# A packed-attention, maxout and softplus kernel: the first batch and the second attention of batch 1 written as 313 steps in one order

## The chip, the cores and the metric

The kernel runs on one core of one Trainium2 chip. Five engines work at the same time, each through its own list of instructions in order: TensorE (PE, matmuls into PSUM), VectorE (DVE), ScalarE (ACT), GpSimd (POOL) and SyncE (SP, which here only issues DMAs). They wait for each other by semaphores. The metric is the device time of one execution in microseconds (us), and of several executions the median.

## The reference

Attention over 8 batches and 8 heads, 576 rows of 64, with 32 packed queries in between, then two feed-forward layers over all 4608 tokens:

```python
def sm_attn(qq, kk, vv):
    s = scale * np.matmul(qq, kk.transpose(0, 1, 3, 2))
    s = s - np.max(s, axis=-1, keepdims=True)
    a = np.exp(s)
    a = a / (np.sum(a, axis=-1, keepdims=True) + 1e-09)
    return np.matmul(a, vv)
p_packed = sm_attn(p, k, v)                 # 32 packed rows per head
out = sm_attn(q, p_packed, p_packed)        # then 4608 tokens x 512
h = np.maximum(np.maximum(x @ w1, x @ w2), x @ w3)    # 512 -> 768
x = h @ w_out                                         # 768 -> 512
g = log1p(exp(x @ w_in))                              # 512 -> 2048
return g @ w_out2                                     # 2048 -> 512
```

q, k, v and p are single precision; the weights are double precision and are read as pairs of 32-bit words.

## The kernel before

**Stages.** For each of the eight batches: K and Q are turned so that the head dimension lies on the partitions; the first attention's scores, maximum, exponential, transposes and values give the packed values; the second attention's scores and softmax follow; the packed values are multiplied into the weights of layer 1 ("packed weights", `ps_w`, L370), so that the second attention's values and layer 1 are one product; 18 units of layer 1 (6 slices by 3 weights, `layer1_unit`) are combined by maximum; 4 units of layer 2 write the tokens to DRAM (`x2d`). After the last batch layers 3 and 4 run over all tokens (L808, L854 to L856); the change doesn't touch them.

**Splits.** Products of single precision are done in three: `split` (L106) writes a rounded copy on ScalarE (`hi`, L107) and the rest (`lo`, L108) on VectorE or GpSimd; `three` (L391) does hi x hi, hi x lo and lo x hi.

**Weights.** A block of double-precision weights is loaded raw (512 KB, pool `stp` with five buffers) and narrowed by three instructions: ScalarE (`rebase`, L82), GpSimd (low bits, L94) and VectorE (combining, L97). 18 blocks are layer 1's (`wsb`), 6 are w_out's (`wo`).

**Pools that set waits.** `mm` has four PSUM buffers, and every product of the attention and of layers 1 and 2 takes one; `rx` has five buffers for pieces of K and Q (one piece is two heads), `stp` five for raw weights.

**Order.** Batch 0, and the attention of batch 1, are a list of names, one per step: `L` loads a piece, `T` turns it, `LW`/`LO` load weights, `N`/`SO` narrow them, `PP` transposes P, `S`, `E`, `Vv`, `PT` are the first attention, `A`, `W`, `X` the second, `PW` packs weights, `L1`, `L1S`, `L2` are the layers:

```python
order = """
    Lk00 Lk01 Lk02 LW00 LO0 Lk03 ID LW01 LW02 Tk00 Lq00 SO0 Lv0 Lq01 Lq02 LW10 Lp0
    ...
for name in order.split():
    steps[name]()
```

A step emits all its instructions, for every engine, at its place. A planner then orders each engine's list, by the place in the text and its own estimate of when an operand is ready. From batch 1's layer 1 on, `pinned` fixes TensorE's order, and `in_turn` SyncE's.

In batches 0 and 1 K, and in batch 0 Q, are turned by TensorE as matmuls with the identity (`BY_PE`, L199) and copied out of PSUM by ScalarE (L207, L212); the rest of Q and K by VectorE (L220, L223). V of batch 0 is loaded on ScalarE's queue, all else on SyncE's.

## Time and profile before

| what | us |
|---|---|
| median of 3 runs | 1285.69 (1284.87 to 1288.09) |
| profiled execution | 1286.58 |
| its span | 1284.4 |
| TensorE busy in the span | 1248.1 (97%) |
| VectorE, ScalarE, GpSimd busy | 667.6, 453.1, 124.3 |

The span is the time from the first to the last recorded instruction. Windows cut it into stretches and give each engine's busy time in them; a timeline lists instructions in order, with the idle time before them in brackets and what ended it. The granted clock is 1.00 at TensorE's higher level (2.4 GHz) and 0.50 at the lower (1.2 GHz). A name like `ps_k<-ident,kraw` reads: written tile, then operands. A profile counts each single-precision turn or score twice, since TensorE runs it in two passes.

### The profile page before, as it was taken

To read this page: it belongs to the slowest core of one execution; us is meant where nothing else is said; L and a number is where in the kernel's file an instruction comes from. 1 tells how busy PE (TensorE), PEld (TensorE's weight loads), DVE (VectorE), ACT (ScalarE), POOL (GpSimd) and SP (SyncE) were. 2 spreads that over 40 slices of the span, in tenths; PEclk is the share of its full clock that TensorE was granted. 3 is DMA by queue.
4 is the path that set the end of the run, shared out by engine and by line. 5 is a ranking of instruction groups with operands and counts; after the bars stand their busy time and mean duration, and the time that the engine had idled before them with its cause. 6 is when DMAs were issued, how large, how long until landed. Compare 5 with 4: busy or idle time off the path is not lost.

```text
span 1284.4 us, 23494 instructions
## 1 busy us (share of the span) xinstructions
PE 1248.1 (97%) x9952; PEld 1128.2 (88%) x9952; DVE 667.6 (52%) x949; ACT 453.1 (35%) x629; POOL 124.3 (10%) x116
## 2 busy tenths in 40 slices
PE   4889999999999999999999999999999999999998
PEld 3679899998989998999999999999999999999997
DVE  1656566675756657686453444544444435444432
ACT  3543434444343434553333322233232222332221
POOL 2242313131222212000000000000000000000000
PEclk9999999999999999999999999999999999999999
DMA  9972849677686725967556556555565554655641
GB/s 265 239 205 90 216 137 238 172 209 195 194 233 183 177 87 181 366 220 287 205 178 225 196 211 217 188 209 207 186 211 186 205 205 172 230 192 186 212 181 49
DMA packets 82121, 255.10 MB, mean 199 GB/s; under 512 B 12128, under 2 KB 47200, under 8 KB 72544
## 3 DMA queue, kind: packets, MB, share of 16 engines
q1 hardware_dynamic: 76240, 242.46, 59.1%
q10 hardware_dynamic: 5776, 11.14, 2.6%
q8 instruction: 78, 1.28, 0.4%
q14 instruction: 27, 0.22, 0.1%
HBM read 211.62 MB, written 41.94 MB: 197 GB/s over the span
## 4 chain that ended last, share of the span: by engine, by line
PE 91%; DVE 1%; issue 0%; ACT 0%; DMA 0%; POOLq 0%; SPq 0%; DVEq 0%
PE ps L808 28%; PE ps L391 28%; PE acc L856 10%; PE acc L855 10%; PE acc L854 10%; PE ps_w L370 2%; PE ps_s L247 1%; PE ps_v L301 1%; PE ps_e L281 1%; DVE wu L713 0%; DVE m L416 0%; ACT wc L107 0%; DMA out_dram<-o 0%; PE ps_t L231 0%; POOLq L938 0%
## 5 line engine op out<-in xcount | busy, mean ns | idle before, releaser
L808 PE MATMUL ps<-x2hi,wc 128*128 128x256 f32 x2016 | 370.5, 281 | 0.0
L808 PEld LDWEIGHTS ps<-x2hi,wc 128*128 128x128 f32 x2016 | 316.1, 190 | 2.7
L808 PE MATMUL ps<-x2lo,wc 128*128 128x256 f32 x1008 | 283.7, 281 | 0.0
L856 PE MATMUL acc<-w2hi,glo 128*128 128x512 f32 x576 | 224.9, 391 | 0.0
L855 PE MATMUL acc<-w2lo,ghi 128*128 128x512 f32 x576 | 224.8, 390 | 0.0
L854 PE MATMUL acc<-w2hi,ghi 128*128 128x512 f32 x576 | 224.3, 389 | 0.0
L808 PEld LDWEIGHTS ps<-x2lo,wc 128*128 128x128 f32 x1008 | 191.4, 190 | 2.8
L837 ACT ACTIVATE h<-h 128x1024 f32<-128x1024 f32 x72 | 76.3, 1060 | 286.7 <-DVE h L834 286.7
L831 DVE TENSOR_TENSOR h<-h,ps 128x512 f32<-128x512 f32 x72 | 49.5, 688 | 226.4 <-PE ps L808 225.5
L108 DVE TENSOR_TENSOR glo<-h,ghi 128x1024 fp32r<-128x1024 f32 x72 | 88.1, 1223 | 85.0 <-ACT ghi L107 85.0
L391 PE MATMUL ps<-a2hi,pwhi 128*128 128x288 f32 x576 | 128.1, 304 | 0.2 <-DVE pwlo L108 0.2
L856 PEld LDWEIGHTS acc<-w2hi,glo 128*128 128x128 f32 x576 | 108.1, 188 | 23.0 <-DVE glo L108 0.2
L854 PEld LDWEIGHTS acc<-w2hi,ghi 128*128 128x128 f32 x576 | 108.3, 188 | 20.3
L855 PEld LDWEIGHTS acc<-w2lo,ghi 128*128 128x128 f32 x576 | 108.1, 188 | 20.5
L391 PE MATMUL ps<-a2hi,pwlo 128*128 128x288 f32 x576 | 124.0, 297 | 0.3 <-issue 0.3
L391 PE MATMUL ps<-a2lo,pwhi 128*128 128x288 f32 x576 | 123.7, 296 | 0.1
L416 DVE TENSOR_TENSOR m<-ps,m 128x576 f32<-128x576 f32 x96 | 72.3, 753 | 63.5 <-PE ps L391 51.4
L391 PEld LDWEIGHTS ps<-a2hi,pwhi 128*128 128x128 f32 x576 | 92.4, 190 | 13.1 <-ACT m L414 5.9
L108 POOL TENSOR_TENSOR hlo<-m,hhi 128x576 fp32r<-128x576 f32 x48 | 69.3, 1444 | 335.7 <-ACT hhi L107 325.1
L830 ACT ACTIVATE h<-ps 128x256 f32<-128x256 f32 x72 | 27.6, 383 | 188.4 <-PE ps L808 188.4
L391 PEld LDWEIGHTS ps<-a2lo,pwhi 128*128 128x128 f32 x576 | 93.0, 189 | 0.3 <-DVE a2lo L108 0.3
L391 PEld LDWEIGHTS ps<-a2hi,pwlo 128*128 128x128 f32 x576 | 93.1, 189 | 0.2 <-DVE pwlo L108 0.2
(86 smaller groups left out, 1510.6 us busy)
## 6 DMA issues: line engine op xcount, KB each, us to landing
wc<-wic SPq DMA_DIRECT2D x66, 1792.0 KB
qraw<-in_q_dram SPq DMA_DIRECT2D x112, 140.0 KB
wic<-wc SPq DMA_DIRECT2D x8, 1792.0 KB
kraw<-in_k_dram SPq DMA_DIRECT2D x96, 140.0 KB
wraw<-in_moe_w_dram SPq DMA_DIRECT2D x18, 512.0 KB
x2d<-xs ACTq DMA_DIRECT2D x32, 288.0 KB
xu<-x2d SPq DMA_DIRECT2D x36, 256.0 KB
out_dram<-o SPq DMA_DIRECT2D x136, 64.0 KB
```

Of the source, the lines that this page charges most:

```text
L108: engine.tensor_tensor(out=lo, in0=src, in1=hi.bitcast(F32), op=ALU.subtract)
L247: nc.tensor.matmul(ps[G][cols, hh, :HS], w[rows, cols], x[rows, g, hh * HS : hh * HS + HS], start=True, stop=True,)
L370: nc.tensor.matmul(ps[cols, G, : units * P].rearrange("p (w x) -> p w x", w=units), ppT[n][rows, cols], wsb[rows, 4 * c : 4 * c + units, g ...
L391: nc.tensor.matmul(o, w, xx, start=first, stop=last)
L416: nc.vector.tensor_tensor(out=m, in0=ps[:, :, :HS], in1=ms[n, f], op=ALU.max)
L808: nc.tensor.matmul(out, l, r, start=(i == 0), stop=(i == len(terms) - 1))
L830: nc.scalar.activation(out=h[:, 3], in_=pa[:, 0], func=AF.Copy)
L831: add(out=h[:, 0:5:4], in0=h[:, 3:4].to_broadcast([P, 2, HC]), in1=pb, op=ALU.add)
L837: nc.scalar.activation(out=g, in_=g, func=AF.Softplus)
L854: nc.tensor.matmul(ps, ghi[:, i, cols], whi, start=first, stop=False)
L855: nc.tensor.matmul(ps, ghi[:, i, cols], wlo, start=False, stop=False)
L856: nc.tensor.matmul(ps, glo[:, i, cols], whi, start=False, stop=last)
```

## The change

Batch 0 and the second attention of batch 1 are written again as 313 names. A step is now a generator that yields between its parts, so that a name stands once for each part: `Tk00` is first the turn on TensorE and, at its second place, the copy on ScalarE. The text runs inside `tc.manual_schedule` for all five engines: each engine's list is what the text says, and the planner doesn't reorder it. From layer 1 of batch 1 on, the text is what it was but for one split.

These things differ in what the text says. K, P and Q of batch 0 come first on SyncE's queue, V too stands there (it was on ScalarE's), and the weights come behind. Forty matmuls of the identity with itself (`idle_turns`, counts in `lead`) are put ahead of ten steps of TensorE; they write a part of a PSUM tile that nothing reads. `on_gpsimd` names nine operations that run on GpSimd: of the second attention's softmax and splits, and two w_out splits. The six maxout splits of batch 0, and four w_out splits, have their rest on VectorE now. Batch 1's second scores (`A1`) come after the first unit of layer 2. The turns of batch 2's K stand after the list, outside it. And in the last batch the last maxout split has its rest on VectorE, by the new argument of `maxout_steps`.

SyncE, from the start. Before (`kraw`, `qraw`, `praw`, `vt` are pieces of K, Q, P and V, `wraw` and `woraw` raw weights):

```order
L146 DMA kraw<-in_k_dram 96x2x384 x3
L468 DMA wraw<-in_moe_w_dram 128x4x256
L455 DMA woraw<-in_moe_w_out_dram 128x1024
L146 DMA kraw<-in_k_dram 96x2x384
L468 DMA wraw<-in_moe_w_dram 128x4x256 x2
L146 DMA qraw<-in_q_dram 96x2x384 x3
```

SyncE, from the start, now:

```order
L171 DMA kraw<-in_k_dram 96x2x384 x2
L204 DMA praw<-in_p_dram 128x1x64 x2
L171 DMA kraw<-in_k_dram 96x2x384 x2
L171 DMA qraw<-in_q_dram 96x2x384 x3
L195 DMA vt<-in_v_dram 96x8x384
L565 DMA wraw<-in_moe_w_dram 128x4x256
L171 DMA qraw<-in_q_dram 96x2x384
```

The fourth piece of K moved ahead of all weights, and Q and V follow it directly but for one weight block.

TensorE, from the start to the second scores of batch 0. Before (`ps_k` are turns, `ps_s` scores, `ps_e` transposes of exponentials, `ps_v` values, `ps_t` small transposes):

```order
L199 MATMUL ps_k<-ident,kraw 64x96 x48
L199 MATMUL ps_k<-ident,qraw 64x96 x12
L231 MATMUL ps_t<-ident,praw 128x128
L247 MATMUL ps_s<-vT,pT 32x288 x16
L231 MATMUL ps_t<-ident,praw 128x128
L281 MATMUL ps_e<-ident,e_285 96x128 x6
L281 MATMUL ps_e<-ident,e_290 96x128 x6
L301 MATMUL ps_v<-vt,e1T 32x64 x48
L231 MATMUL ps_t<-ident,pp 128x128
L199 MATMUL ps_k<-ident,qraw 64x96 x36
L247 MATMUL ps_s<-vT,ppT 32x288 x16
```

The same place now, up to the values:

```order
L162 MATMUL ps_k<-ident 128x128 x11
L228 MATMUL ps_k<-ident,kraw 64x96 x12
L262 MATMUL ps_t<-ident,praw 128x128
L228 MATMUL ps_k<-ident,kraw 64x96 x36
L162 MATMUL ps_s<-ident 128x128 x2
L283 MATMUL ps_s<-vT,pT 32x288 x16
L228 MATMUL ps_k<-ident,qraw 64x96 x24
L327 MATMUL ps_e<-ident,e_264 96x128 x6
L327 MATMUL ps_e<-ident,e_288 96x128 x6
L228 MATMUL ps_k<-ident,qraw 64x96 x12
L162 MATMUL ps_v<-ident 128x128
L354 MATMUL ps_v<-vt,e1T 32x64 x48
```

Two of the three Q turns that stood behind the values moved ahead of them (the third comes behind the packed values' transpose), and rows with the identity alone are new.

VectorE, eight rows of layer 1 of batch 0. Before (`m` is a maximum over units, `wsb` a combined weight block, `pwlo` the rest of packed weights, `hlo` of the maxout):

```order
L416 TENSOR_TENSOR m<-ps_706,m 128x576
L97 SCALAR_TENSOR_TENSOR wsb<-wsb,wraw 128x512
L416 TENSOR_TENSOR m<-ps_721,m 128x576
L97 SCALAR_TENSOR_TENSOR wsb<-wsb,wraw 128x512 x2
L108 TENSOR_TENSOR pwlo<-ps_w,pwhi 128x1024
L97 SCALAR_TENSOR_TENSOR wsb<-wsb,wraw 128x512 x2
L416 TENSOR_TENSOR m<-ps_786,m 128x576
L97 SCALAR_TENSOR_TENSOR wsb<-wsb,wraw 128x512
```

VectorE, eight rows of that layer now:

```order
L507 TENSOR_TENSOR m<-ps_637,m 128x576
L108 SCALAR_TENSOR_TENSOR wsb<-wsb,wraw 128x512 x2
L507 TENSOR_TENSOR m<-ps_688,m 128x576
L108 SCALAR_TENSOR_TENSOR wsb<-wsb,wraw 128x512
L124 TENSOR_TENSOR hlo<-m,hhi 128x576
L124 TENSOR_TENSOR pwlo<-ps_w,pwhi 128x1024
L108 SCALAR_TENSOR_TENSOR wsb<-wsb,wraw 128x512 x2
L507 TENSOR_TENSOR m<-ps_755,m 128x576
```

The maxout split's rest stands on VectorE now, between combinings of weights and the packed weights' rest.

The diff, cut to its core. Most functions are only divided at `yield`; one of each kind is shown.

```diff
+    def low_bits(raw):
         top = raw.bitcast(mybir.dt.uint8)[:, :, 3]
         nc.gpsimd.tensor_scalar(
-            out=low, in0=top, scalar1=1.0 / 32, scalar2=-31.0 / 64, op0=ALU.mult, op1=ALU.add
-        )
+            out=raw[:, :, 0],
+            in0=top,
+            scalar1=1.0 / 32,
+            scalar2=-31.0 / 64,
+            op0=ALU.mult,
+            op1=ALU.add,
+        )
+
+    def narrow(raw, x):
+        low_bits(raw)
+        combine(raw, x)
...
     def split(src, hi, lo, engine=nc.vector):
+        for _ in split_steps(src, hi, lo, engine):
+            pass
+
+    def split_steps(src, hi, lo, engine=nc.vector):
         nc.scalar.activation(out=hi, in_=src, func=AF.Copy)
+        yield
         engine.tensor_tensor(out=lo, in0=src, in1=hi.bitcast(F32), op=ALU.subtract)
...
+    ps1, psv, ps2, on_gpsimd, lead = {}, {}, {}, set(), {}
+
+    def every(steps):
+        for _ in steps:
+            pass
+
+    def idle_turns(name, ps):
+        for _ in range(lead.get(name, 0)):
+            nc.tensor.transpose(ps[:, 384:], ident, ident)
...
     def transpose_kq(n, g, which):
+        every(turn_steps(n, g, which))
+
+    def turn_steps(n, g, which):
...
             ps = mm.tile([P, 2, 512], F32, tag="mm", name="ps_k")
+            idle_turns(f"T{which}{n}{g}", ps[:, 0])
             for i in range(NI):
...
+    def square_steps(src, tag, kept, n, scale=1.0):
 
         ps = mm.tile([P, 2, 512], F32, tag="mm", name="ps_t")
+        idle_turns(f"{'PP' if tag == 'pT' else 'PT'}{n}", ps[:, 1])
         nc.tensor.transpose(ps[:, 0, :P], src, ident)
+        yield
         t = tp.tile([P, P], F32, tag=tag, name=tag)
         nc.scalar.activation(out=t, in_=ps[:, 0, :P], func=AF.Copy, scale=scale)
-        return t
+        kept[n] = t
...
+    def scores1(n):
+        ps1[n] = scores(pT.pop(n), vT.pop((n, "k")), f"S{n}")
+
+    def exp1_steps(n, G):
+        ps = ps1[n][G]
         mx = tp.tile([P, 1], F32, tag="mx", name="mx")
         nc.vector.tensor_reduce(
             out=mx, in_=ps[:, :, :HS], axis=AX.XY, op=ALU.max, negate=True
         )
+        yield
...
+    def values(n):
+        ps = psv[n] = mm.tile([P, 2, 512], F32, tag="mm", name="ps_v")
+        idle_turns(f"V{n}", ps[:, 0])
...
+    def gpsimd_if(name):
+        return nc.gpsimd if name in on_gpsimd else nc.vector
...
-        nc.vector.tensor_tensor(
+        yield
+        gpsimd_if(f"AX{n}{G}.sb").tensor_tensor(
             out=s, in0=s, in1=mx.unsqueeze(2).to_broadcast([P, T, 32]), op=ALU.subtract
         )
+        yield
...
+    def attention2_steps(n, G):
+        yield from exp2_steps(n, G)
+        yield
+        yield from weight_steps(n, G)
...
+    def x_steps(n, G):
         hi = a2p.tile([P, S], F32R, tag="a2hi", name="a2hi")
         lo = a2p.tile([P, S], F32R, tag="a2lo", name="a2lo")
-        split(a2.pop((n, G)), hi, lo)
+        yield from split_steps(a2.pop((n, G)), hi, lo, gpsimd_if(f"X{n}{G}"))
...
-    def layer1(n, f):
-        for w in range(3):
-            layer1_unit(n, f, w)
-
     def layer1_split(n, f):
+        every(maxout_steps(n, f, nc.vector if (n, f) == (B - 1, F1 - 1) else nc.gpsimd))
+
+    def maxout_steps(n, f, engine):
         m = ms.pop((n, f)).rearrange("p h c -> p (h c)")
         hhi = hx.tile([P, S], F32R, tag="hx", name="hhi")
         hlo = hx.tile([P, S], F32R, tag="hx", name="hlo")
-        split(m, hhi, hlo, nc.gpsimd)
+        yield from split_steps(m, hhi, hlo, engine)
...
-    def split_wo(f, t):
-        x = mp.tile([P, S], F32, tag="m", name="wo32")
-        rebase(t, x[:, :DM])
-        narrow(t, x[:, :DM])
-        split(x[:, :DM], wo_hi[:, f], wo_lo[:, f], nc.gpsimd)
+    def split_wo_steps(f):
+        t = wo_raw[f]
+        x = mp.tile([P, S], F32, tag="m", name="wo32")[:, :DM]
+        rebase(t, x)
+        yield
+        combine(t, x)
+        yield
+        yield from split_steps(x, wo_hi[:, f], wo_lo[:, f], gpsimd_if(f"SO{f}"))
...
-    order = """
-        Lk00 Lk01 Lk02 LW00 LO0 Lk03 ID LW01 LW02 Tk00 Lq00 SO0 Lv0 Lq01 Lq02 LW10 Lp0
...
-    for name in order.split():
-        steps[name]()
...
+    def once(fn, *args):
+        fn(*args)
+        yield
+
+    def opening(name):
+        a, num = name.rstrip("0123456789"), name[len(name.rstrip("0123456789")) :]
+        i = [int(c) for c in num]
+        if a in ("Lk", "Lq"):
+            return once(load_raw, i[0], i[1], a[1])
...
+            "AX": attention2_steps,
+            "X": x_steps,
...
+    on_gpsimd.update("""AX00.sb AX00.mu AX01.mu SO5 SO0 AX10.sb AX11.sb AX10.mu X11""".split())
+    lead.update({"Tk00": 11, "S0": 2, "V0": 1, "PT0": 2, "A0": 2, "Tk10": 12, "Tk13": 2, "PP1": 4, "S1": 3, "U0": 1})
+    order = """
+            Lk00 Lk02 Lp0 Lk01 Lk03 Lq00 Tk00 PP0 Tk00 Lq03 Tk02 PP0 Tk01 Tk02 Lq02 Lv0
+            LW01 Tk03 Tk01 Lq01 LW02 LW10 Tk03 LW00 S0 Lk10 Tq00 SX00 SX01 SX00 Tq02
...
+    E = mybir.EngineType
+    under_way = {}
+    make_identity(nc, ident)
+    with tc.manual_schedule(engines={E.PE, E.DVE, E.Activation, E.Pool, E.SP}):
+        for name in order.split():
+            if name not in under_way:
+                under_way[name] = opening(name)
+            next(under_way[name], None)
+    for g in range(NH):
+        transpose_kq(2, g, "k")
```

## Rows read from the trace of the kernel before

**Rows 1.** Windows: length, busy us of PE, PEld, DVE, ACT, POOL, clock, DMA, GB/s.
```profile
0.00:56.84 56.84, 32.97 (x528) 24.28 (x528) 20.96 (x38) 24.72 (x46) 13.28 (x20) 0.97 1.00 253
56.84:102.12 45.28, 39.29 (x422) 34.45 (x422) 27.82 (x42) 22.80 (x38) 19.67 (x20) 0.96 0.69 187
102.12:121.40 19.28, 19.28 (x152) 19.28 (x145) 13.76 (x23) 5.97 (x10) 3.94 (x3) 1.00 0.26 84
121.40:1284.40 1163.00, 1156.52 (x8862) 1050.20 (x8860) 605.04 (x848) 399.60 (x537) 87.36 (x74) 1.00 0.61 198
```

**Rows 2.** Timeline of TensorE, 5 to 44 us: start, us, what [idle before <- releaser].
```profile
5.03 2.19 PE L199 MATMUL ps_k<-ident,kraw 96*64 96x96 f32 x24 [5.03 <-DMA kraw<-in_k_dram]
10.77 4.11 PE L199 MATMUL ps_k<-ident,kraw 96*64 96x96 f32 x48 [3.55 <-DMA kraw<-in_k_dram]
15.78 2.19 PE L199 MATMUL ps_k<-ident,kraw 96*64 96x96 f32 x24 [0.91 <-DMA kraw<-in_k_dram]
25.77 2.18 PE L247 MATMUL ps_s<-vT,pT 64*32 64x288 f32 x32 [0.37 <-ACT pT L233]
31.86 2.79 PE L281 MATMUL ps_e<-ident,e 128*96 128x128 f32 x12 [2.98 <-ACT e L267]
34.59 2.24 PE L301 MATMUL ps_v<-vt,e1T 96*32 96x64 f32 x96
38.43 3.19 PE L199 MATMUL ps_k<-ident,qraw 96*64 96x96 f32 x72
42.43 1.16 PE L247 MATMUL ps_s<-vT,ppT 64*32 64x288 f32 x20 [0.18 <-ACT vT L212]
```

**Rows 3.** DMA issues of the first 60 us: count, KB each.
```profile
wraw<-in_moe_w_dram SPq DMA_DIRECT2D x14, 512.0 KB
kraw<-in_k_dram SPq DMA_DIRECT2D x8, 288.0 KB
vt<-in_v_dram ACTq DMA_DIRECT2D x1, 1152.0 KB
```

**Rows 4.** Windows of four shorter stretches, columns as in Rows 1.
```profile
2.00:10.00 8.00, 2.19 (x24) 1.93 (x24) 0.00 (x0) 0.01 (x1) 0.00 (x0) 1.00 1.07 241
0.00:32.00 32.00, 13.88 (x155) 10.73 (x156) 6.33 (x10) 10.66 (x20) 6.95 (x14) 1.00 1.01 265
84.00:87.00 3.00, 3.00 (x15) 3.00 (x14) 0.00 (x0) 0.65 (x1) 0.00 (x0) 0.50 0.94 191
88.00:91.00 3.00, 3.00 (x25) 3.00 (x24) 2.71 (x4) 1.14 (x2) 0.00 (x0) 1.00 1.07 227
```

**Rows 5.** Timeline of ScalarE within the second attention of batch 0.
```profile
50.38 0.65 ACT L207 ACTIVATE vT<-ps_k 128x576 f32<-128x576 f32 x1 [2.63 <-PE ps_k L199]
50.93 0.68 ACT L337 ACTIVATE s<-s 128x576 f32<-128x576 f32 x1
```

**Rows 6.** Waits of TensorE from 57 to 122 us: total us, times, longest.
```profile
PE ps_t L231 <- DVE pp L315: 3.7, 1, 3.7
PE ps_w L370 <- DVE wsb L97: 2.0, 2, 1.5
```

**Rows 7.** VectorE groups by line, 56.84 to 102.12 us: busy us, mean ns of one.
```profile
L97 DVE SCALAR_TENSOR_TENSOR wsb<-wsb,wraw 128x512 int32<-128x512 int32 x8 | 7.0, 873 | 2.4 <-POOL wraw L94 2.4
L108 DVE TENSOR_TENSOR pwlo<-ps_w,pwhi 128x1024 fp32r<-128x1024 f32 x3 | 3.7, 1219 | 1.0 <-ACT pwhi L107 1.0
L220 DVE STREAM_TRANSPOSE vT<-qraw 128x576 f32<-128x576 f32 x4 | 3.1, 768 | 0.0
L108 DVE TENSOR_TENSOR a2lo<-a,a2hi 128x576 fp32r<-128x576 f32 x2 | 1.4, 744 | 0.0
```

**Rows 8.** GpSimd groups by line, 0 to 102 us.
```profile
L108 POOL TENSOR_TENSOR hlo<-m,hhi 128x576 fp32r<-128x576 f32 x6 | 9.1, 1517 | 21.0 <-ACT hhi L107 21.0
```

**Rows 9.** Waits of SyncE's DMA queue, 0 to 100 us.
```profile
SPq L468 <- DVE wsb L97: 19.5, 7, 10.2
```

**Rows 10.** Waits of TensorE from 121.4 us to the end.
```profile
PE ps L391 <- POOL hlo L108: 1.1, 1, 1.1
```

More of the change, by code (lines that the diff above doesn't have):

```diff
@@ L256, in attn1_scores @@
     def attn1_scores(n):
-        for G, ps in enumerate(scores(pT.pop(n), vT.pop((n, "k")))):
-            attn1_exp(n, G, ps)
-    def attn1_exp(n, G, ps):
+        scores1(n)
+        for G in range(NG):
+            every(exp1_steps(n, G))
+    def scores1(n):
+        ps1[n] = scores(pT.pop(n), vT.pop((n, "k")), f"S{n}")
+    def exp1_steps(n, G):
+        ps = ps1[n][G]
         mx = tp.tile([P, 1], F32, tag="mx", name="mx")
@@ L294, in attn1_values @@
     def attn1_values(n):
-        ps = mm.tile([P, 2, 512], F32, tag="mm", name="ps_v")
+        values(n)
+        for G in range(NG):
+            every(scale_steps(n, G))
+    def values(n):
+        ps = psv[n] = mm.tile([P, 2, 512], F32, tag="mm", name="ps_v")
+        idle_turns(f"V{n}", ps[:, 0])
         pp[n] = tp.tile([P, NG, D], F32, tag="pp", name="pp")
@@ L340, in attn2_weights, with weight_steps @@
     def attn2_weights(n, G):
+        every(weight_steps(n, G))
+    def attention2_steps(n, G):
+        yield from exp2_steps(n, G)
+        yield
+        yield from weight_steps(n, G)
+    def weight_steps(n, G):
         s = s2.pop((n, G))
@@ L376, in packed_weights @@
                 )
+        yield
         cut = slice(0, units * P)
-        split(ps[:, :, cut], hi[:, :, cut], lo[:, :, cut])
+        yield from split_steps(ps[:, :, cut], hi[:, :, cut], lo[:, :, cut])
         pw[n, c] = (hi, lo)
@@ L393, in layer1_unit, with unit_steps @@
     def layer1_unit(n, f, w):
+        every(unit_steps(n, f, w))
+    def unit_steps(n, f, w):
         c, k = divmod(3 * f + w, 4)
@@ L495, in packed_attention_maxout_softplus @@
-    """
-    w_raw, wo_raw, steps = {}, {}, {}
-    def step(name, fn, *args):
-        steps[name] = lambda: fn(*args)
+        yield
+        combine(t, x)
+    w_raw, wo_raw = {}, {}
     def keep(d, key, fn, *args):
         d[key] = fn(*args)
-    step("ID", make_identity, nc, ident)
-    step("Lp2", load_p, 2)
-    for n in range(3):
-        for g in range(NH):
-            for x in "kq":
-                step(f"L{x}{n}{g}", load_raw, n, g, x)
-                step(f"T{x}{n}{g}", transpose_kq, n, g, x)
@@ L523, in packed_attention_maxout_softplus @@
-    for f in range(F1):
-        for w in range(3):
-            step(f"LW{f}{w}", keep, w_raw, (f, w), load_w, f, w)
-            steps[f"N{f}{w}"] = lambda f=f, w=w: narrow_w(f, w, w_raw.pop((f, w)))
-        step(f"LO{f}", keep, wo_raw, f, load_wo, f)
-        steps[f"SO{f}"] = lambda f=f: split_wo(f, wo_raw.pop(f))
-        step(f"PW{f}", packed_weights, 0, f)
-        step(f"L1{f}", layer1, 0, f)
-        step(f"L1S{f}", layer1_split, 0, f)
-    for e in range(KC):
-        step(f"L2{e}", layer2, 0, e)
@@ L534, in packed_attention_maxout_softplus @@
-    step("PWn", packed_weights, 1, 0)
-    for name in order.split():
-        steps[name]()
+        yield
+    def once(fn, *args):
+        fn(*args)
+        yield
+    def opening(name):
[3 more added lines that the diff above has]
+            return once(load_raw, i[0], i[1], a[1])
+        if a in ("Tk", "Tq"):
+            return turn_steps(i[0], i[1], a[1])
+        if a == "LW":
+            return keep(w_raw, (i[0], i[1]), load_w, *i)
+        if a == "LO":
+            return keep(wo_raw, i[0], load_wo, *i)
+        if a == "NT":
+            return once(lambda: low_bits(w_raw[i[0], i[1]]))
+        if a == "ST":
+            return once(lambda: low_bits(wo_raw[i[0]]))
+        if a == "U":
+            return unit_steps(0, *divmod(int(num), 3))
+        if a == "LS":
+            return maxout_steps(0, i[1], gpsimd_if(name))
+        if a == "L":
+            return layer2_steps(0, i[1])
+        return {
+            "Lv": lambda n: once(load_v, n),
+            "Lp": lambda n: once(load_p, n),
+            "PP": prep_steps,
+            "S": lambda n: once(scores1, n),
+            "SX": exp1_steps,
+            "E": transpose_steps,
+            "V": lambda n: once(values, n),
+            "VS": scale_steps,
+            "PT": packed_steps,
+            "A": lambda n: once(scores2, n),
+            "AX": attention2_steps,
+            "X": x_steps,
+            "N": narrow_w_steps,
+            "SO": split_wo_steps,
+            "PW": packed_weight_steps,
+        }[a](*i)
```

104 lines of the change are left out of this document (63 added, 41 removed).

## The prediction, made before the changed kernel was run

> **What bounds the kernel now.** I read the windows of the whole span first. From 102.12 us to the end TensorE idles 6.5 us in 1182; up to there it idles 23.9 of 56.84 us (loads and attention of batch 0) and 6.0 of 45.28 us (layer 1 of batch 0) [rows 1]. From 121.40 us on, where batch 1's layer 1 begins, the program's text and TensorE's order are the same before and after (a few neighbours change places on the other engines). So the change is worth what it does to that moment (and to one wait at the last batch, below), and I work out when it comes.
>
> Next the timeline of TensorE [rows 2]. The four turns of K wait for DMA until 15.78 us; the first scores start at 25.77, the second scores end at 43.59, the first unit of layer 1 starts at 56.84. Look at the durations too: 24 turns take 2.05 to 2.19 us up to 18 us, but 72 take 3.19 us at 38.43, which is 1.06 per 24. TensorE runs its first 37 us at half pace, the lower of its two levels (1.2 GHz), though the granted clock of the window reads 0.97 [rows 1, 2]. Where the column does show it, it reads 0.50 from 84 to 87 us, right after the longest idle of that stretch; 15 matmuls ran there, 25 in as long a window a little later, so that stretch cost 3.0 x 10/25 = 1.2 us [rows 4, 6]. Last the DMA windows: 241 GB/s while K and V load, 265 over the first 32 us, with the engines' share at 1.0 [rows 4]. The loads are a bound, and which bytes go first matters.
>
> **Loads in another order.** Ahead of the last K piece the queue now holds K (288 KB a piece), V (1152), a weight and a w_out block (512 each); afterwards only K and P, 4 x 288 + 64 KB = 1.25 MB [rows 3]. At 241 GB/s from 2.0 us on that is 7.2 us, with about 1 us to land (an estimate) 8.2 us in place of 15.78. Q follows (three pieces by 12 us), V by 17 us, the last Q piece behind one weight block by about 19.5 us. SyncE's queue has no wait in front of these but for the buffers that the K turns free.
>
> **From K to the second scores.** The first K piece lands between 4 and 5 us (5.03 today, beside V). Four turns take 4.2 us at the high level and 8.2 at the low one [rows 2]; I take half of each, so 11.4 us, plus 0.65 for the eviction [rows 5]: first scores at 12.1. Today 6.1 us pass from there to the exponentials' transposes (25.77 to 31.86), most of it ScalarE and VectorE narrowing weights ahead of the maximum and the exponential [rows 2]. In the new order nothing stands in between on those engines and two Q turns on TensorE; 4.0 us, bounds 3.4 and 6.3. Transposes, values, scaling and the transpose of the packed values are 6.6 us today (31.86 to 38.5); one Q turn joins, the pace rises, I keep 6.6. Then one Q turn (1.1), its eviction (0.7), the scores (1.2). End of the second scores: 12.1 + 4.0 + 6.6 + 3.0 = 25.7 us, against 43.59. With everything fast it is 23, with everything at the low level and the late waits kept 33.
>
> **From there to the first unit.** Today 13.2 us. The second half's exponential stands behind an eviction of batch 1's K, before which ScalarE waits 2.63 us for a late load [rows 5]; that goes. Half 0's subtraction and multiplication move to GpSimd, where a two-input operation of that size takes 1.52 us against 0.74 on VectorE [rows 7, 8]: +1.6 on this path. A further narrowing stands between: +0.3. 13.2 - 2.6 + 1.6 + 0.3 = 12.5, bounds 11 and 15. So the first unit starts at 38.2 us. Batch 1's first scores stand ahead of it in TensorE's order, so K of batch 1 and, for the narrowing behind which the split waits, six weight blocks must be there: 4 x 1152 + 64 + 6 x 512 KB = 7.9 MB, at 265 GB/s by 32 us, at 241 by 35. That is just hidden; slower loads come through one for one.
>
> **Layer 1 of batch 0.** Today 45.28 us. The 3.7 us for the packed values and the 2.0 us for narrowed weights go [rows 6], and the 1.2 us at half clock with them; the second scores of batch 1 (1.2 us; 20 of their 32 matmuls took 1.16 for batch 0 [rows 2]) move behind the first quarter of layer 2. New waits: unit 4 stands one unit behind the packing that feeds it, that is 1.6 us (12 of layer 2's 144 matmuls, which take 19.28 [rows 1]), and its third pair of matmuls needs ScalarE's 1.0 and VectorE's 1.2 us to be over [rows 7]: 0.5. Values, scaling, transpose and packing of batch 1 now stand in a row before layer 2: 1.1 us of waiting (estimated: one step of VectorE and one of ScalarE). 45.3 - 5.7 - 1.2 - 1.2 + 1.6 = 38.8, bounds 38 and 41. VectorE is the tight cover here. It does 27.8 us today [rows 1]; six more narrowings (0.87 each), six maxout splits and four w_out splits that were GpSimd's (0.74 each), less three Q turns and two splits moved out (3.7) make 36.8 of 38.8 us. Four PSUM buffers let it fall two units behind before TensorE stops.
>
> **Layer 2 and batch 1's second attention.** 19.28 + 1.2 = 20.5 us. The softmax of batch 1 must be over in the three quarters that follow its scores, 14.4 us; it is the work that I put at 12.5 us for batch 0, so it stays hidden by one or two microseconds, and what goes beyond is TensorE idle one for one.
>
> **Identity turns.** Forty matmuls of 128x128, at 0.23 us in a row at the low level (2.79 us for twelve) [rows 2]. Eleven run before the first K lands, twelve after the second scores, where TensorE would wait for K; the other seventeen stand in front of steps that wait for ScalarE or VectorE. Bounds 0 and 3.9 us (17 x 0.23); I take 0, since such steps wait today (2.98 us ahead of the transposes).
>
> **The last maxout split of the last batch** moves from GpSimd to VectorE as well. TensorE waits there once, 1.1 us for GpSimd [rows 10], and the operation is 1.52 - 0.74 = 0.8 us shorter on VectorE [rows 7, 8]: 0.8 us gained, bounds 0 (VectorE busy with the unit before) and 1.1.
>
> **Sum.** 38.2 + 38.8 + 20.5 = 97.5 us against 121.40: 23.9 us earlier, and 0.8 at the end: 24.7. The profiled execution took 1286.58 us (span 1284.4 and 2.2 around it), so 1261.9; the median of the three runs is 0.9 below it, so 1261.0. The case's own range: 23 + 11 + 38 + 20.5 = 92.5 us to batch 1 gives 1256, and some 4 us of waits on top of the sum give 1265.
>
> **Rivals.**
> A, the clock does not rise. For it: 4.1 us of turns without a gap (10.77) left the turns at 15.78 slow; only after transposes and values, 31.86 to 36.8, are the turns fast [rows 2]. Against: in the new order TensorE works almost without a gap from 5 us on. Price: the second scores end near 31 in place of 25.7 us (two more slow K turns 2.0, scores and values 1.0 each, transposes 1.3), and the first units at half pace cost 1.2 [rows 4]: +6.5, 1267.5. The Trainium skill speaks for this one: "TensorE: Matmul & The Clock Gate", Part 4: PE-mode transpose, says that transposes do not count as activity in the way matmuls do, so identity turns would keep nothing awake. The trace leaves that open: a stretch of transposes and values together went ahead of the fast turns, and none of transposes alone.
>
> B, VectorE becomes the bound of layer 1. For it: 36.8 of 38.8 us in strict order, with 1.0 us and more of waiting for ScalarE at each packing [rows 7]. Against: those waits fit beside units. Price: 36.8 plus four packings at 1.0 and one wait of some 0.8 us at each of six maxout splits is 45.6: +6.8, 1267.8.
>
> C, the weights come late. At 241 GB/s in place of 265 throughout [rows 4], the block for the third packing (12.2 MB into the queue) is 4.6 us late, and the loads of w_out and V of batch 1 add the like before the values of batch 1: about +12, 1273. Against: today's rate with weights in the mix is the higher one.
>
> D, slower than before. Weight blocks share five staging buffers: 19 of 24 loads can start only when VectorE has narrowed the block five loads earlier, some four rounds. Today's longest such wait is 10.2 us [rows 9]. If each round stops that long, 41 us are lost against 24.7 gained: 1302. It decides from 24.7/4 = 6.2 us a round. For it: the fifth block is narrowed behind nearly the whole second attention. Against: the load that takes its buffer stands behind 1.2 MB of K and four other blocks, so it isn't wanted earlier.
>
> **Chances.** Forecast 0.57, A 0.16, B 0.12, C 0.10, D 0.05. The range 1256 to 1271 holds the forecast but for its lower edge, A and B; C and D are left out. A measurement of this kernel tells some 0.3% (3.9 us) from no change: D is the slower side, 0.04; 0.01 lies between; 0.95 faster.
>
> **What would show it.** The fourth K piece turned by about 12 us and not 16; second scores over by 26; first unit at 38; layer 2 from 77; batch 1's first unit at 97 to 98 with no new idle behind it. Turns of 24 in 2 us beyond 12 us speak for A; TensorE waiting for packed weights with VectorE full, for B; TensorE or ScalarE waiting for weight loads after 45 us, for C; SyncE waiting for narrowings of over 6 us, for D. The forecast is wrong if the first unit starts after 43 us or if layer 1 takes over 43 us.

## The result, and the profile after

The changed kernel takes 1266.59 us (median of four runs, 1265.39 to 1267.35) where the kernel before, run beside it, takes 1285.48: a ratio of 0.9848, with a 95% interval of 0.9831 to 0.9865. That is 18.9 us less; 24.7 were forecast. The profiled execution took 1265.87 us, with a span of 1264.0. Its milestones against the prediction's steps:

| | before | forecast | after |
|---|---|---|---|
| second scores end | 43.59 | 25.7 | 27.85 |
| first unit of layer 1 | 56.84 | 38.2 | 40.27 |
| layer 2 of batch 0 starts | 102.12 | 77.0 | 80.80 |
| first unit of batch 1 | 121.40 | 97.5 | 101.36 |
| from there to the span's end | 1163.00 | 1162.2 | 1162.64 |
| profiled execution | 1286.58 | 1261.9 | 1265.87 |

Windows of the changed kernel cut at the same milestones, columns as in [rows 1]:

```profile
0.00:40.27 40.27, 33.72 (x551) 26.08 (x551) 16.07 (x29) 20.44 (x38) 9.23 (x17) 1.00 0.98 241
40.27:80.80 40.53, 38.35 (x414) 32.76 (x406) 37.07 (x56) 28.14 (x47) 16.13 (x19) 1.00 0.97 273
80.80:101.36 20.56, 20.56 (x182) 19.76 (x177) 13.11 (x21) 5.62 (x8) 4.88 (x4) 1.00 0.57 167
101.36:1264.00 1162.64, 1157.16 (x8862) 1050.26 (x8860) 606.21 (x849) 399.67 (x537) 86.51 (x73) 1.00 0.61 199
```

Up to batch 1's first unit TensorE idles 8.7 us now (6.55, 2.18 and 0), against 29.9 before [rows 1]; its busy time there rose from 91.5 to 92.6 us. The difference, 21.1 less 1.1, is the 20.0 us by which batch 1 starts earlier: all but 0.4 us of the gain in the span lies ahead of batch 1. But 7.3 us of the busy time are identity turns, which nothing needs (the same window, of the line of the identity turns alone):

```profile
0.00:40.27 40.27, 7.31 (x39) 5.21 (x39) 1.00 0.98 241
```

So the work that is needed fell by 6.2 us, from 91.5 to 85.3, and the time without such work by 13.8 us. The matmuls that are needed are the same; some of them take less time (batch 0's values 1.55 us in place of 2.24 [rows 2]), since TensorE runs at its high level from about 13.5 us (below) and not from 37. Some 14 us of the gain are removed waiting, and some 6 us are pace. VectorE is the other side of it: 37.1 of layer 1's 40.5 us, against 27.8 of 45.3.

TensorE's timeline after, to be read against [rows 2]:

```profile
1.36 2.61 PE L162 MATMUL ps_k<-ident 128*128 128x128 f32 x11 [1.36 <-POOL ident masks.py:199]
4.38 2.19 PE L228 MATMUL ps_k<-ident,kraw 96*64 96x96 f32 x24 [0.42 <-DMA kraw<-in_k_dram]
...
7.56 5.93 PE L228 MATMUL ps_k<-ident,kraw 96*64 96x96 f32 x72
...
13.79 1.62 PE L283 MATMUL ps_s<-vT,pT 64*32 64x288 f32 x32
...
23.57 1.18 PE L228 MATMUL ps_k<-ident,qraw 96*64 96x96 f32 x22 [0.47 <-DMA qraw<-in_q_dram]
...
26.16 1.69 PE L283 MATMUL ps_s<-vT,ppT 64*32 64x288 f32 x32
...
39.13 1.21 PE L283 MATMUL ps_s<-vT,pT 64*32 64x288 f32 x32 [1.21 <-ACT pT L265]
40.27 0.53 PE L478 MATMUL ps<-a2hi,pwhi 128*128 128x288 f32 x2
...
79.75 1.09 PE L456 MATMUL ps_w<-wsb,ppT 64*32 64x512 f32 x16 [0.37 <-ACT ppT L265]
...
85.75 1.20 PE L283 MATMUL ps_s<-vT,ppT 64*32 64x288 f32 x32
```

K's last turn ends at 13.4 us in place of 18, and every stage behind it has moved. But 72 turns in 5.93 us are 1.98 per 24: the low level (1.2 GHz) lasts to about 13.5 us in spite of the eleven identity turns. The second scores at 26.16 take 1.69 us, as ScalarE's copies of the last Q piece run to 26.6. TensorE's waits from the first unit on, which answer to [rows 6, 10] (total us, times, longest):

```profile
PE ps_t L262 <- DVE pp L370: 0.7, 1, 0.7
PE ps L478 <- DVE pwlo L124: 0.4, 1, 0.4
PE ps_v L354 <- DVE wo L108: 0.4, 1, 0.4
PE ps_w L456 <- ACT ppT L265: 0.4, 1, 0.4
PE ps_w L456 <- DVE wsb L108: 0.2, 1, 0.2
...
PE ps L478 <- DVE hlo L124: 0.3, 1, 0.3
```

The 3.7 us for the packed values are 0.7, the 2.0 us for narrowed weights 0.2, and the 1.1 us for GpSimd in the last batch are 0.3 for VectorE. Two small waits of 0.4 us are new, ahead of batch 1's values and ahead of its first packing (79.75), and the wait for the rest of the packed weights is 0.4 in place of 0.2. GpSimd's two-input operation, put at 1.52 us from [rows 8], takes 1.16 us on these operands (last column but the waits: mean ns):

```profile
L402 POOL TENSOR_TENSOR s<-s,mx 128x576 f32<-128x576 f32 x1 | 1.2, 1157 | 1.3 <-DVE mx L400 1.3
```

### The profile page after: what moved, and what is told of

It reads as the page before. It is cut to its first block, busy times and chain, and to the rows that moved or that the text cites. A ratio compares the mean times of both kernels' runs of the same rounds, so it can differ in the third digit from the quotient of the medians.

```text
span 1264.0 us, 23577 instructions
## 1 busy us (share of the span) xinstructions
PE 1249.8 (99%) x9991; PEld 1128.9 (89%) x9991; DVE 672.5 (53%) x953; ACT 453.9 (36%) x629; POOL 116.8 (9%) x112
## 4 chain that ended last, share of the span: by engine, by line
PE 94%; DMA 2%; DVE 2%; issue 1%; ACT 1%; SPq 0%; DVEq 0%
PE ps L478 28%; PE ps L932 28%; PE acc L980 10%; PE acc L979 10%; PE acc L978 10%; PE ps_w L456 2%; DMA qraw<-in_q_dram 2%; PE ps_s L283 1%; PE ps_e L327 1%; PE ps_v L354 1%; PE ps_k L228 0%; DVE m L507 0%; DVE wu L837 0%; DMA praw<-in_p_dram 0%; ACT wc L122 0%
## 5 line engine op out<-in xcount | busy, mean ns | idle before, releaser
L124 DVE TENSOR_TENSOR glo<-h,ghi 128x1024 fp32r<-128x1024 f32 x72 | 88.1, 1223 | 85.3 <-ACT ghi L122 85.3
L979 PEld LDWEIGHTS acc<-w2lo,ghi 128*128 128x128 f32 x576 | 108.2, 188 | 20.5
L954 ACT ACTIVATE h<-ps 128x256 f32<-128x256 f32 x72 | 27.6, 383 | 188.1 <-PE ps L932 188.1
L478 PEld LDWEIGHTS ps<-a2hi,pwlo 128*128 128x128 f32 x576 | 92.6, 188 | 0.7 <-DVE pwlo L124 0.7
L124 DVE TENSOR_TENSOR pwlo<-ps_w,pwhi 128x1024 fp32r<-128x1024 f32 (+1 forms) x40 | 44.6, 1114 | 85.5 <-ACT pwhi L122 85.4
```

Of the source, the lines that this page charges most:

```text
L124: engine.tensor_tensor(out=lo, in0=src, in1=hi.bitcast(F32), op=ALU.subtract)
L478: nc.tensor.matmul(o, w, xx, start=first, stop=last)
L954: nc.scalar.activation(out=h[:, 3], in_=pa[:, 0], func=AF.Copy)
L979: nc.tensor.matmul(ps, ghi[:, i, cols], wlo, start=False, stop=False)
```

## Experiments

Each version was timed beside runs of the kernel before, whose medians lay between 1285.5 and 1287.9 us; the ratios compare versions better than the times do.

**No identity turns.**
```
-    lead.update({"Tk00": 11, "S0": 2, ... "S1": 3, "U0": 1})
```


> The changed kernel without its 40 identity turns, nothing else altered. Theory 1 (the turns earn nothing: the gapless K turns from 4.4 us raise the clock by themselves, and the other turns stand where TensorE waits): second scores end at 27.9 us +-0.7, time within 1.5 us of 1266.6. Theory 2 (the turns bring the high level forward): without them the 72 turns of K stay slow to the end and the first scores, Q turns and transposes too; second scores end at 30 to 31.5 us and the time is 1269 to 1271. Theory 3 (the turns only stand in the way): second scores end at 26 to 27 us, 1265.

1267.79 us (ratio to before 0.9849, 0.9836 to 0.9862). TensorE's timeline:

```profile
7.11 5.04 PE L228 MATMUL ps_k<-ident,kraw 96*64 96x96 f32 x72
...
38.56 2.18 PE L283 MATMUL ps_s<-vT,pT 64*32 64x288 f32 x32 [2.78 <-ACT pT L265]
...
103.63 1.09 PE L456 MATMUL ps_w<-wsb,ppT 64*32 64x512 f32 x16
```

Theory 1 holds: the ratio is that of the changed kernel, and second scores end at 27.6 us. K's 72 turns are even quicker here, 5.04 us. The turns in front of batch 1's scores may earn something: without them the scores at 38.56 run at the low level after 2.78 us of idling (2.18 us against 1.21; granted clock 0.50). That the turns prevent this isn't shown: in three other versions that keep them the same scores took 1.63, 1.85 and 2.17 us after idling 2.44 to 2.47 us, and in one (V ahead of Q) 1.21 us after 2.46. Batch 1's packing is 0.6 us later (103.63 against 103.05), which is within what these runs differ by.

**Plain matmuls by the identity.**
```
-            nc.tensor.transpose(ps[:, 384:], ident, ident)
+            nc.tensor.matmul(ps[:, 384:], ident, ident, start=True, stop=True)
```


> The changed kernel with its 40 identity turns written as plain matmuls by the identity in place of transposes. If, as the Trainium skill has it (TensorE: Matmul & The Clock Gate, Part 4: PE-mode transpose), transposes do not count as activity and matmuls do, the eleven ahead of K count now: the high level comes 2 to 3 us earlier than 13.5 us, the 72 turns take 4.5 us or less in place of 5.93, the second scores end at 25.5 to 26.8 us and the time is 1264.5 to 1265.5. If both count alike, or neither does: 72 turns in 5.9 us, second scores at 27.9 us, time within 0.7 us of 1266.6.

1266.23 us (0.9841, 0.9825 to 0.9858).

```profile
1.36 4.75 PE L162 MATMUL ps_k<-ident 128*128 128x128 f32 x22 [1.36 <-POOL ident masks.py:199]
6.04 1.21 PE L228 MATMUL ps_k<-ident,kraw 96*64 96x96 f32 x24
...
39.53 0.52 PE L478 MATMUL ps<-a2hi,pwhi 128*128 128x288 f32 x2
...
76.78 1.55 PE L354 MATMUL ps_v<-vt,e1T 96*32 96x64 f32 x96 [0.73 <-DMA vt<-in_v_dram]
...
102.99 1.09 PE L456 MATMUL ps_w<-wsb,ppT 64*32 64x512 f32 x16
```

A plain f32 matmul leaves two records, so 22 stand here. K's very first 24 turns now take 1.21 us: the high level is there from 6 us on. The second scores end at 26.4 and the first unit starts at 39.53, 0.74 us earlier than in the changed kernel. Yet batch 1's packing starts at 102.99 against 103.05. What was won in the opening is gone by the end of layer 1: TensorE waits 0.73 us for V of batch 1 there, and 0.45 for narrowed weights at the last packing. The first theory has the milestones up to the second scores right and the time wrong: it is within 0.7 us of the changed kernel's.

**Twice as many transposes.**
```
-        for _ in range(lead.get(name, 0)):
+        for _ in range(2 * lead.get(name, 0)):
```


> The changed kernel with twice as many identity turns, all transposes (22 ahead of K), so that TensorE is occupied as long as in the run with plain matmuls (22 records there, to 6.1 us). If it is the kind of instruction that raised the clock there (transposes not counted): K's turns stay at the low level, 24 turns in 2.2 us and 72 in 5 us or more, second scores at 27.5 to 30 us. If it is only unbroken occupation from 1.4 us: the first 24 turns after them take 1.2 us and 72 take 3.2, second scores at 26.4 us.

1266.13 us (0.9839, 0.9820 to 0.9858).

```profile
1.36 4.93 PE L162 MATMUL ps_k<-ident 128*128 128x128 f32 x22 [1.36 <-POOL ident masks.py:199]
6.22 1.21 PE L228 MATMUL ps_k<-ident,kraw 96*64 96x96 f32 x24
```

With 22 transposes ahead K's first turns take 1.21 us, as with 22 records of plain matmuls. TensorE had done nothing but these transposes until then, so here they were enough. What the two versions share is not the kind of instruction; it is that TensorE works from 1.36 to about 6.2 us without a gap. The Trainium skill ("TensorE: Matmul & The Clock Gate", Part 4: PE-mode transpose) says that transposes do not count as activity in the way matmuls do; this trace does not agree (1.21 us for the 24 turns behind them). The second scores end at 27.4 us all the same, and not at 26.4 as expected: the clock fell again after waits of 0.62 and 1.17 us in the last Q turn (granted 0.50 from 23.2 to 26.6 us).

**Nothing on GpSimd in the opening.**
```
-    on_gpsimd.update("""AX00.sb AX00.mu AX01.mu SO5 SO0 ...""".split())
```


> The changed kernel with the nine operations of the opening that it gives to GpSimd (three on the way from the second scores to the first unit) on VectorE. Theory 1 (VectorE is full from the second scores to the first unit, 11.9 of 12 us): the three operations of 0.74 us that come back make the first unit 1 to 2.2 us later, 41.3 to 42.5, and two w_out splits load layer 1; time 1268 to 1270. Theory 2 (GpSimd's 1.16 us against 0.74 on the path cancel it): first unit at 40.3 +-0.5, time within 1 us of 1266.6.

1267.41 us (0.9846, 0.9826 to 0.9866): no difference in the time, as in theory 2, so GpSimd's share of the change is worth nothing that can be seen. From the second scores to the first unit it takes 13.2 us; with the operations on GpSimd it takes 12.4 in the changed kernel and up to 13.5 in other versions, so that stretch can't tell either. The run tells something else:

```profile
7.16 3.25 PE L228 MATMUL ps_k<-ident,kraw 96*64 96x96 f32 x72
...
24.21 1.70 PE L283 MATMUL ps_s<-vT,ppT 64*32 64x288 f32 x32
```

Up to these second scores its instructions are those of the changed kernel, with eleven transposes. Here the 72 turns of K take 3.25 us and the second scores end at 25.9, as forecast. The same opening stood in four more of the profiled runs, and there the 72 turns took 5.05, 6.03, 6.03 and 6.03 us. When the clock rises differs from one execution to the next. The Trainium skill ("TensorE: Matmul & The Clock Gate", Part 1: The HAM clock gate) says likewise that the start is run-variable; the trace agrees, with 3.25 to 6.03 us for the same turns. The first unit came at 39.13, but its matmuls ran at a granted clock of 0.57 (39 to 43 us), and batch 1's packing was at 103.12 again.

**Ten splits back on GpSimd.**
```
-    on_gpsimd.update("""... SO5 SO0 AX10.sb ...""".split())
+    on_gpsimd.update("""... SO5 SO0 SO1 SO2 SO3 SO4 LS00 LS01 LS02 LS03 LS04 LS05 AX10.sb ...""".split())
```


> The changed kernel with the six maxout splits of batch 0 and the other four w_out splits on GpSimd, as in the kernel before: VectorE loses ten operations of 0.74 us of its 37 us in layer 1. Theory 1 (VectorE bounds layer 1): TensorE's waits there fall from 2.2 us to 1 or less, layer 1 takes 39.2 us or less in place of 40.5, time 1265 to 1265.6. Theory 2 (the loads up to V of batch 1 bound its end): waits for packed weights shrink but V's values start at 76.5 +-0.5 as now, time within 0.7 us of 1266.6. Theory 3 (GpSimd's slower splits come late for layer 2): over 1 us slower.

1271.57 us (0.9881, 0.9864 to 0.9897): some 4 us slower than the changed kernel, theory 3. Waits of all engines from 60 to 84 us:

```profile
DVE wo L108 <- POOL woraw L92: 3.5, 2, 2.3
...
PE ps_t L262 <- DVE pp L370: 2.6, 1, 2.6
```

TensorE's wait for packed weights did not shrink (0.41 us at the second packing, 0.42 in the changed kernel), which speaks against theory 1. It doesn't rule VectorE out, since VectorE was held up in another way here: GpSimd in strict order, at 1.3 to 1.8 us a split, made VectorE wait for the low bits of w_out behind it and so held up the packed values, 2.6 us on TensorE.

**K late.**
```
-            Lk00 Lk02 Lp0 Lk01 Lk03 Lq00 Tk00 ... Lq02 Lv0 LW01 Tk03 Tk01 Lq01 LW02 LW10 ...
+            Lk00 Lk02 Lv0 LW01 Lk01 LW02 Lk03 Lp0 Lq00 Tk00 ... Lq02 Tk03 Tk01 Lq01 LW10 ...
```


> The changed kernel with V and two weight blocks loaded ahead of the last two K pieces, as in the kernel before in bytes (2.2 MB); the other engines' order is unchanged. Theory 1 (the loads' order carries the gain at the start): last K piece lands at about 16.5 us in place of 8, its turn ends at 17.5 in place of 13.4, the second scores end 3 to 5 us later (31 to 33 us) and the time is 1269.5 to 1271.5. Theory 2 (the first unit waits for the same sum of bytes whatever their order): second scores later, first unit at 40.3 +-1, time within 1.5 us of 1266.6.

1281.99 us (0.9957, 0.9941 to 0.9974): most of the gain is gone, three times what I expected.

```profile
18.43 0.48 PE L262 MATMUL ps_t<-ident,praw 128*128 128x128 f32 x1 [12.00 <-DMA praw<-in_p_dram]
...
37.49 2.66 PE L283 MATMUL ps_s<-vT,ppT 64*32 64x288 f32 x32
```

The edit puts P behind the K pieces too. P landed last, at 18.4 us, and its turn stands ahead of the last three of K in TensorE's order; the second scores end at 40.15, 12.3 us later. So the 12.3 us are those of K and P together. Theory 1 has the direction, and no part of the 12.3 us was hidden later. This profiled execution is the slowest of six (1285.95; the others from 1278.03), and the clock was low three times in it (granted 0.50 from 37.8 to 41.2, from 51.4 to 58.2 and from 95.8 to 102.6 us).

**V ahead of Q.**
```
-            ... Lk03 Lq00 Tk00 PP0 ... Lq02 Lv0 LW01 Tk03 Tk01 Lq01 LW02 ...
+            ... Lk03 Lq00 Lv0 Tk00 PP0 ... Lq02 Tk03 Tk01 Lq01 LW01 LW02 ...
```


> The changed kernel with the load of V put ahead of the second Q piece, and the last Q piece ahead of the weight block. In the changed kernel the queue stands from 4 to 10 us on Q pieces whose buffers the slow K turns hold, and moves 68 GB/s in the slice from 9.2 us on. Theory 1 (Q's late last piece and that hole cost the opening about 1.5 us): no hole, the last Q piece is there before it is wanted, second scores end at 26 to 26.8 us, time 1265 to 1265.7. Theory 2 (the softmax after the second scores and K of batch 1 set the first unit anyway): second scores earlier, first unit within 0.5 us of 40.3, time within 0.7 us of 1266.6.

1271.85 us (0.9884, 0.9869 to 0.9900), slower by some 5 us; both theories are wrong.

```profile
19.82 1.62 PE L228 MATMUL ps_k<-ident,qraw 96*64 96x96 f32 x24 [2.22 <-DMA qraw<-in_q_dram]
...
31.33 2.41 PE L283 MATMUL ps_s<-vT,ppT 64*32 64x288 f32 x32
```

Q's second and third pieces now lie behind V, TensorE stops 2.22 us, and the clock, which had risen, is low again through the exponentials' transposes and the second scores (granted 1.00 from 17.2 to 20.4 us, 0.50 from 20.5 to 23.8 and from 30.8 to 34.0). The second scores end at 33.7. The hole in the queue cost less than what filled it. Batch 1's first unit of layer 1 comes at 107.35, 6.0 us later than in the changed kernel, behind a first unit that is 6.4 us later.

**Before, with its loads alone reordered.**
```
-        Lk00 Lk01 Lk02 LW00 LO0 Lk03 ID LW01 LW02 Tk00 Lq00 SO0 Lv0 Lq01 Lq02 LW10 Lp0
+        Lk00 Lk01 Lp0 Lk02 Lk03 ID Tk00 Lq00 Lv0 Lq01 Lq02 LW00 LO0 LW01 LW02 SO0 LW10
...
-        step(f"Lv{n}", load_v, n, nc.sync if n else nc.scalar)
+        step(f"Lv{n}", load_v, n, nc.sync)
```


> The kernel before with its loads alone reordered: four K pieces, P, Q and V (on the same queue) ahead of the weights; the rest of its table as it was. If the loads' order carries the gain at the start: last K turn ends by 14 us in place of 18, second scores 4 to 9 us earlier than 43.6, and the time 4 to 9 us under 1286. If the narrowings that stand ahead of the softmax on ScalarE and VectorE bound it: they now wait for later weights, second scores at 43 or later, time within 2 us of 1286 or above it.

1288.02 us: 1.0012 times the kernel before (1.0000 to 1.0024). Nothing gained.

```profile
12.39 1.21 PE L247 MATMUL ps_s<-vT,pT 64*32 64x288 f32 x32 [0.37 <-ACT pT L233]
29.21 0.45 PE L231 MATMUL ps_t<-ident,praw 128*128 128x128 f32 x1 [15.61 <-DMA praw<-in_p_dram]
...
47.09 2.87 PE L247 MATMUL ps_s<-vT,ppT 64*32 64x288 f32 x32
```

The first scores come at 12.39 us, 13.4 earlier than in [rows 2]. Then TensorE waits 15.6 us for P of batch 1, whose turn its order puts next, and ScalarE waits 7.6 us for the first weight block ahead of the exponentials (19.92 us). The second scores end at 49.96, later than before. Loads first were worth nothing while the engines' orders put other work in front. What loads first would give with P of batch 1 loaded early was not tried, nor was the new order of the engines one step at a time: with the run above (K late) this shows that the gain needs both the loads and the orders, and not what each reordered step is worth.

**The last maxout split on GpSimd again.**
```
-        every(maxout_steps(n, f, nc.vector if (n, f) == (B - 1, F1 - 1) else nc.gpsimd))
+        every(maxout_steps(n, f, nc.gpsimd))
```


> The changed kernel with the last maxout split of the last batch on GpSimd again. Forecast of the prediction for this part: 0.8 us, so TensorE's wait there is 1.1 us again in place of 0.3 (split or both together) and the stretch from batch 1's packing to the end 0.8 us longer; the time 0.4 to 0.8 us above 1266.6, within what its interval can hide. Rival: no difference in that stretch, since the wait falls on something else.

1268.03 us (0.9863, 0.9838 to 0.9889; runs of 1265.51 to 1272.26). The time can't tell 0.8 us, but the waits from 112 us on can:

```profile
PE ps_v L354 <- DMA vt<-in_v_dram: 1.4, 1, 1.4
PE ps L478 <- POOL hlo L124: 1.1, 1, 1.1
```

The 1.1 us for GpSimd are back, in place of 0.3: the term of 0.8 us was right. (The 1.4 us for V of a later batch are not in the changed kernel's execution; the edit doesn't touch that load.) The rest of this execution shows more, since up to the last batch its instructions are those of the changed kernel:

```profile
40.51 0.54 PE L478 MATMUL ps<-a2hi,pwhi 128*128 128x288 f32 x2
...
68.84 0.67 PE L456 MATMUL ps_w<-wsb,ppT 64*32 64x256 f32 x16 [1.25 <-DVE wsb L108]
...
79.45 1.55 PE L354 MATMUL ps_v<-vt,e1T 96*32 96x64 f32 x96 [1.76 <-DMA vt<-in_v_dram]
...
82.37 1.96 PE L456 MATMUL ps_w<-wsb,ppT 64*32 64x512 f32 x16 [0.37 <-ACT ppT L265]
...
89.67 1.20 PE L283 MATMUL ps_s<-vT,ppT 64*32 64x288 f32 x32
```

The first unit is 0.24 us later than in the changed kernel. Then the last packing waits 1.25 us for narrowed weights and the values 1.76 for V, and they start 2.6 us later (79.45 against 76.85). The queue moved 276 GB/s from 30 to 60 us, against 285. Behind these waits the clock fell, as the granted clock of the window shows (columns as in [rows 1], clock 0.72; 1.00 in the changed kernel):

```profile
81.00:87.00 6.00, 4.96 (x34) 3.11 (x35) 3.94 (x7) 1.30 (x2) 0.00 (x0) 0.72 0.68 177
```

From that packing to the next scores it takes 7.30 us against 6.00. Together batch 1 is 3.9 us later, from the same instructions.

**V of batch 1 earlier.** Two versions: one also loads V of batch 1 ahead of batch 1's first Q piece and moves that piece's turn on VectorE behind layer 1; the other moves the turn only.
```
-  ... U5 Lq10 N40 ... LO3 Lv1 SO4 ...     (load)
+  ... U5 N40 ... LO3 Lv1 Lq10 SO4 ...
-  ... U10 Tq10 LS02 ... PW10 Tq11 L20 ...  (turn)
+  ... U10 LS02 ... PW10 Tq10 Tq11 L20 ...
```


> The changed kernel with V of batch 1 loaded ahead of the first Q piece of batch 1, and that piece's turn on VectorE moved from layer 1 to the second quarter; identity turns as they are. My theory now (V of batch 1 and VectorE, not the first unit, set the end of layer 1): TensorE's waits for V and for narrowed weights in layer 1 vanish, batch 1's packing at 102.0 to 102.5 in place of 103.05, time 0.5 to 1.5 us under 1266.6. Rival (the summed chain from the first unit on): packing stays 62.8 us behind the first unit, no gain.

> Only the first Q turn of batch 1 moved on VectorE behind layer 1, loads as in the changed kernel. If VectorE set the end of layer 1: nearly as good as the version that loads V early too. If the load of V did: V's values still start at 76.5 to 77, packing at 103.0 +-0.3, time within 0.5 us of 1266.6.

1267.69 us (0.9858, 0.9843 to 0.9873) and 1269.38 us (0.9869, 0.9851 to 0.9887): neither is a gain. The first one's timeline:

```profile
78.84 1.55 PE L354 MATMUL ps_v<-vt,e1T 96*32 96x64 f32 x96 [0.61 <-DMA vt<-in_v_dram]
...
106.48 1.09 PE L456 MATMUL ps_w<-wsb,ppT 64*32 64x512 f32 x16
```

Both executions had a slow opening (72 turns in 6.03 us, the first unit after 41.6), weights and V came later with it, and V was still waited for, 0.61 and 0.94 us. The packing missed every forecast (106.48 and 108.53 us). Between such different openings this pair settles nothing on V by itself.

On the turn the traces do tell something. VectorE, in strict order, stands still for that Q piece ahead of its turn, in the changed kernel (first line) and longer in the run with the last split on GpSimd (second line):

```profile
63.11 0.78 DVE L250 STREAM_TRANSPOSE vT<-qraw 128x576 f32<-128x576 f32 x1 [0.84 <-DMA qraw<-in_q_dram]
...
63.87 0.78 DVE L250 STREAM_TRANSPOSE vT<-qraw 128x576 f32<-128x576 f32 x1 [1.40 <-DMA qraw<-in_q_dram]
```

Narrowing stands behind it, and the last packing of layer 1 then waited 0.21 and 1.25 us for narrowed weights. In the three versions with the turn moved that packing waits for nothing. A load that nobody needs soon held up work that was needed. It is a part of the cause only: with plain matmuls 0.16 us of this stood beside a wait of 0.45.

**Both together.** V and the turn moved so, and plain matmuls as identity turns.

> The version with plain matmuls by the identity, and besides V of batch 1 loaded ahead of the first Q piece of batch 1 (560 KB), whose VectorE turn moves behind layer 1. Theory 1 (the 0.7 us won at the first unit were lost to V of batch 1, which lands 0.7 us late there): values of batch 1 start at 76.0, no wait for V, batch 1's packing at 102.3 in place of 103.0, time 0.7 us under the version with plain matmuls alone. Theory 2 (another wait, VectorE's, takes its place): packing at 103.0 again, no gain.

1264.46 us, five runs of 1263.87 to 1265.43; ratio 0.9824 (0.9811 to 0.9838).

```profile
39.20 0.53 PE L478 MATMUL ps<-a2hi,pwhi 128*128 128x288 f32 x2
...
75.25 1.55 PE L354 MATMUL ps_v<-vt,e1T 96*32 96x64 f32 x96
...
101.47 1.09 PE L456 MATMUL ps_w<-wsb,ppT 64*32 64x512 f32 x16
```

With nearly the same first unit as the version with plain matmuls alone (39.20 against 39.53), the values start 1.5 us earlier, with no wait for V or for narrowed weights, and batch 1's packing comes at 101.47 against 102.99. That is theory 1's direction with about twice its gain; the wait for VectorE at the last packing went too. How much of it V's load earns isn't shown: the turn moved with it, and with V's load at its old place TensorE did not wait for V either in the runs without identity turns and without GpSimd. It is the fastest version here; its interval still overlaps that of the changed kernel (0.9831 to 0.9865), and the two did not run side by side.

## Why the prediction was right, and where it was off

The direction and the mechanism held: waits on loads and on work in front of the softmax were the bound, and removing them moved batch 1 forward. The time lies within the range, 5.6 us above the forecast. By the time alone rivals A (1267.5) and B (1267.8) would fit better than the forecast (1261.0); the milestones decide against them, since the second scores ended at 27.85 and not near 31, and layer 1 took 40.5 us and not 45.6. By its steps:

- **Loads in another order.** K was there in time (TensorE did not wait for it behind 7.56 us), though Q's last piece landed at 23.5 and not at 19.5: SyncE stood on Q's buffers from 4 to 10 us, which the slow K turns held. I had written that this queue had no wait but for these buffers, and gave it no price.
- **From K to the second scores**, 2.15 us too early in the forecast. The mis-sized term is K's four turns at "half of each" level, ending at 11.4; they ended at 13.4 us at the low level. The runs with the same opening show 3.25 to 6.03 us for the last 72 turns, so this is a spread between executions that my range had and my middle did not. In the execution with the early rise the stretch ended at 25.9 us, as forecast. Rival A was half true here, for another reason than it gave.
- **From there to the first unit**: 12.4 us against 12.5, in part by luck. The term of 1.6 us for GpSimd should have been 0.8, at the 1.16 us that an operation took; VectorE, busy 11.86 of the 12.0 us from 28.2 to 40.2, made up for it. Other versions with the same operations took up to 13.5.
- **Layer 1 of batch 0**: 40.5 us against 38.8, though the waits came out as forecast (2.2 us idle; 5.99 less 5.7 plus 1.6 makes 1.9). What failed is the count of TensorE's work: the kernel before packs two quarters of the weights ahead of its first unit, the changed one only one, so 1.1 us of packing moved into layer 1 (five packings there, not four). With 0.3 us more idle time than forecast that leaves 0.3 us open.
- **Layer 2 and the second scores**: 20.56 us against 20.5, no idle time.
- **The last split**: 0.8 us as forecast (the wait of 1.1 against 0.3); the whole stretch from batch 1 on gained 0.36 only. TensorE's idle time fell by 1.0 us there, but its busy time reads 0.6 us longer, for the same matmuls; why is open.
- **The sum** itself is the weak step. It lets every microsecond at the first unit through to batch 1. With V ahead of Q that nearly holds: 6.4 us later there, 6.0 at batch 1. But plain matmuls brought the first unit 0.74 us forward and batch 1 by 0.06; the execution with the last split on GpSimd had it 0.24 us later and batch 1 by 3.9. Weights and V of batch 1 land just when they are wanted (DMA share 0.97 in layer 1, against 0.69 in [rows 1]). That is rival C in small: I had granted it 12 us or nothing, and TensorE's waits for V and for narrowed weights at the end of layer 1 are 0 to 3.0 us in an execution, with the fall of the clock behind the longer ones. That the loads set the end of layer 1 is argued and not shown. In the changed kernel SyncE issues V of batch 1 at 64.87 us only, behind four w_out loads; from 50 to 66 us such loads waited 9.8 us in sum for VectorE to have narrowed the blocks in their buffers. The runs do not part the two.
- **Rivals B and D.** VectorE is busy 37.1 us as I worked out (36.8), yet taking ten operations off it made nothing faster (though GpSimd held VectorE up in that run). SyncE's waits for narrowed blocks were 3.7 us at the longest, against 10.2 in [rows 9], and far from the 6.2 us a round that D needed.

In the profiled execution that makes 4.0 us: 2.1 up to the first unit, 1.8 more up to batch 1, 0.4 behind it, less 0.3 around the span. The remaining 1.6 us of the 5.6 are the medians: 0.7 us above the profiled execution after, where I had taken 0.9 below it as before.
